# Later scatters, later low parts and shorter scaling turns in a chain of Fourier transform and two expert networks

## The chip, the cores and the metric

One core of a Trainium2 chip runs the whole program. The metric is the device time of one execution in microseconds. The kernel before took 698.27 us (median of three runs, 695.5 to 699.56).

## What is computed

```python
X = np.fft.fft(np.fft.fft(x, axis=1), axis=2).real          # x: (8, 3072, 256)
x = X.reshape(24576, 256)
# first network: 8 experts, weights w1 (8,256,1024), w2 (8,1024,256)
logits = x @ w_gate; P = np.exp(logits - logits.max())
for _ in range(8):
    P /= P.sum(1, keepdims=True) + 1e-09
    P /= P.sum(0, keepdims=True) + 1e-09
    P *= N / E
out = sum(P[:, e:e+1] * (np.maximum(x @ w1[e], 0.0) @ w2[e]) for e in range(8))
# second network, on out: each row goes to the expert of its largest logit
probs = softmax(out @ w_gate2); e = argmax
y[row] = probs[row, e] * (np.maximum(out[row] @ u1[e], 0) @ u2[e])
```

All is float32.

## The kernel before

The transform comes first (`fft_phase`) and leaves its rows in DRAM (`H`). Few rows have a P that is not zero in float32: `route1` finds them, and they are sorted into 30 tiles of 128 rows, three for each of the 8 experts (`CAP = 3`, tiles 0 to 23) and six spare tiles (`NFLAT = 6`, flat tiles 0 to 5) for what does not fit in three. A row that several experts want has copies; the flag `R["prim"]` marks the copy that counts in a column sum, `R["valid"]` the slots that hold a row.

The first network (`moe1`) goes through the experts e = 0 to 7. For each, `Moe.first` (matmuls on L890) makes the hidden layer of 384 rows in 8 groups m, each group in one of four PSUM buffers `ph`; `Moe.relu` takes it out with one ACT instruction (`hh`, L876) and one DVE instruction (`hl`, L427). `Moe.steps` (L923) is the second matrix, one tile t at a time. Every float32 matrix is split in a high part (ACT, L820) and a low part, the rest (`low`, DVE, L826), by `Moe.part`. The three-fold products of the high and low parts give the float32 result. `Moe.turn` transposes the rows of an expert (L843) and splits them as well (`xh` on ACT, `xl` on DVE, L418).

From e = 2 (`F0`) on each expert's stage also takes in one flat tile f = e - 2. Which expert a flat tile belongs to is known on the chip only, so `Free.weights` gathers its weights by index (L792): `fw` (1 MB, first matrix), `rawc` (1 MB, second matrix) and `gd`, three indirect DMAs issued by POOL. Each of the three has one buffer. `Moe.free_first` (L936, 32 matmuls) then reads `fw` at the start of stage e. In the order of POOL's queue the gathers for flat tile f stand at step 5 of stage f + 1.

The results of the first network are summed in DRAM (`acc`). `keep` copies a tile from PSUM into a buffer `y` (L1620), `add` writes it to its own rows by a plain DMA on SP's queue (L1631), and for the first tile of each expert after the first and for every flat tile puts a scatter in a list; `send` takes one entry of this list and issues an indirect DMA with addition on POOL's queue (L797, `acc<-y,Rapos` for a first tile, `acc<-y,Roidx` for a flat one). There are 13 of them. Each waits until the one in front of it has landed, as they touch the same rows. `ADDS` and `SENDS` say at which steps of a stage this happens. Steps are the slots of `Slots`: 0 to 7 behind the groups m of `first`, 8 to 10 in the flat tile's second matrix, 12 on in the three tiles. At (7, 6) and (7, 8) `most` sends what is left.

The scaling of P (`sinkhorn`) runs on DVE on one tile [128, 30, 8] beside stages 2 and 3, in steps that `STEPS` places in the slots: `start`, then eight turns (`cols`, `rows`) each followed by `sums` (L987), a matmul with a matrix of ones that adds the column sums `cs` over the partitions, and `end`, from which the weights `R["wt"]` come.

Behind stage 7 the logits of the sum are read back (`lg<-acc`, L1356), `route2` sorts the rows by expert for the second network, and the rows are gathered from `acc` (`grab2`, six gathers first, three per tile group). `warm` gives PE matmuls on zeros (L1263), so many as its argument says; `W3` are those within `route2` ahead of the matmuls on L550 that make the new row lists `R["gidx"]`. Then come the parts u, 0, 2 and u, 0, 3 of the second network's first expert, the first `turn` of it and `later`, nine small DVE instructions that end in the indices `R["frow"]` of the flat tiles. In `part` a list as last argument keeps the DVE low part, and for odd parts the next fetch of weights into the raw buffers, for later. The second network (`moe2`) has the same stages and writes its rows by indirect DMAs.

Of the kernel before, what the change touches and what calls it, by code (L numbers as in the profile page):

```python
# [12 lines left out]
ALU = mybir.AluOpType  # L13
# [4 lines left out]
NB, S, D, E, FF = 8, 3072, 256, 8, 1024  # L18
# [268 lines left out]
def _consts():  # L287
# [148 lines left out]
class Route:  # L436
# [364 lines left out]
class Moe:  # L801
# [7 lines left out]
    def part(self, r, i, eng, g=None, later=None):  # L809

        nc = self.nc
        if i < 2:
            h = self.w1.tile([128, FF], F32R, name="w1h")
            l = self.w1.tile([128, FF], F32R, name="w1l")
            hv, lv, rv = h, l, r
        else:
            h = self.w2.tile([128, 4, DG], F32R, name="w2h")
            l = self.w2.tile([128, 4, DG], F32R, name="w2l")
            hv, lv, rv = h[:, :, :D], l[:, :, :D], r.rearrange("p (m d) -> p m d", m=4)
        nc.scalar.activation(out=hv, in_=rv, func=AF.Copy)  # L820
        more = i >= 2 and g is not None
        if more:
            nc.scalar.activation(out=h[:, :, D:], in_=g, func=AF.Copy)

        def low():
            eng.tensor_tensor(out=lv, in0=rv, in1=hv.bitcast(F32), op=ALU.subtract)  # L826
            if more:
                eng.tensor_tensor(out=l[:, :, D:], in0=g, in1=h[:, :, D:].bitcast(F32), op=ALU.subtract)  # L828

        if later is None:  # L830
            low()
        else:
            later.append(low)
        return h, l
# [118 lines left out]
def sinkhorn(nc, K, R, pt, pool):  # L953

    o = Ops(nc)
    V = nc.vector
    T = lambda sh, dt=F32, name=None: pool.tile([128] + list(sh), dt, name=name)
    N8 = [128, NTL, 8]
    P, g, pr = T([NTL, 8], name="P"), T([NTL, 8], name="sg_"), T([NTL, 8], name="pr")
    rs, ri, rp, cs, bias = T([NTL], name="rs"), T([NTL], name="ri"), T([NTL], name="rp"), T([8], name="cs"), T([1], name="bias")  # L960
    bc = lambda a: a[:, :, None].to_broadcast(N8)

    def logits(j, X):
        s = slice(CAP * j, CAP * j + CAP)
        o.tt(g[:, s], X[:, :, 129:137], X[:, :, 273:281], ALU.add)
        o.tt(P[:, s], X[:, :, 265:273], R["sg"][:, s, None].to_broadcast([128, CAP, 8]), ALU.mult)
        o.tt(P[:, s], P[:, s], g[:, s], ALU.add)

    def start():
        o.ts(P, P, R["gm"], ALU.subtract)  # L970
        boltz(nc, o, P, g, bias)
        o.tt(P, P, bc(R["valid"]), ALU.mult)

    st = {}

    def rows(it):
        o.red(rs, P, ALU.add)
        o.stt(rs, rs, 1e-9 * (2.0 ** 64 if it == 0 else 1.0), rs, ALU.add, ALU.bypass)
        V.reciprocal(ri, rs)
        o.tt(rp, ri, R["prim"], ALU.mult)  # L980
        o.tt(pr, P, bc(rp), ALU.mult)
        o.red(cs, pr.rearrange("p t e -> p e t"), ALU.add)
        o.tt(P, P, bc(ri), ALU.mult)

    def sums():
        st["pm"] = pt.tile([128, 512], F32, name="pt")
        nc.tensor.matmul(st["pm"][:, 0:8], K["tri"][:, 128:256], cs, start=True, stop=True)  # L987

    def cols():
        o.ts(cs, st["pm"][:, 0:8], 1e-9, ALU.add, 1.0 / (NB * S // E), ALU.mult)  # L990
        V.reciprocal(cs, cs)
        o.tt(P, P, cs[:, None, :].to_broadcast(N8), ALU.mult)

    def end():
        cols()
        o.tt(pr[:, E * CAP:], P[:, E * CAP:], R["sel"], ALU.mult)
        o.red(R["wt"][:, E * CAP:], pr[:, E * CAP:], ALU.add)

        own = P.rearrange("p t e -> p (t e)")[:, :E * (8 * CAP + 1)].rearrange("p (e x) -> p e x", e=E)[:, :, 0:8 * CAP:8]
        o.stt(R["wt"][:, :E * CAP].rearrange("p (e c) -> p e c", e=E), own, 1.0, own, ALU.mult, ALU.bypass)  # L1000
# [12 lines left out]


# [120 lines left out]
F0 = 2  # L1135


def run(tc, ctx, A, out, H, acc, Ld, Pd, Gd, Zd):
    nc = tc.nc
    o = Ops(nc)  # L1140
    P = lambda st, n, b, **k: st.enter_context(tc.tile_pool(name=n, bufs=b, reuse_waits="tile", **k))
# [15 lines left out]
    R = {}  # L1157
# [43 lines left out]
    with tc.manual_schedule():  # L1201
# [27 lines left out]
        with ExitStack() as st:  # L1229
# [38 lines left out]
            def part(s, e, i, eng, later=None):  # L1268
                g = g2[:, e, 4 * (i - 2):4 * (i - 1)] if i > 1 and s == "w" else None
                k = s + "1122"[i], e  # L1270
                W.setdefault((s, e), {})[i] = moe.part(raw[k][:, i % 2], i, eng, g, later)

                def after():
                    raw.pop(k)
                    if (s, e, i) not in HOLD:
                        fetch()
                    if (s, e, i) == ("u", 0, 3):
                        fetch()

                if i % 2:  # L1280
                    after() if later is None else later.append(after)

            with ExitStack() as s1:
# [35 lines left out]
                X = {}  # L1319
# [41 lines left out]
            with ExitStack() as s1:  # L1361
                moe.xp = P(st, "xp2", 2, side="right")
                r2 = P(s1, "r2", 1)
                ring = P(s1, "r2a", 2)
                K["itx"] = r2.tile([128, NTL, NTL], BF16, name="itx2")
                K["irx"] = r2.tile([128, 128, max(CH2)], BF16, name="irx2")
                nc.scalar.activation(out=K["itx"], in_=rt.C("it")[:, :, None].to_broadcast([128, NTL, NTL]), func=AF.Copy)
                nc.scalar.activation(out=K["irx"], in_=rt.C("i128")[:, :, None].to_broadcast([128, 128, max(CH2)]), func=AF.Copy)

                def arrive(choose):  # L1370
                    pg = turned()
                    a, b = E * CAP - CAP + 1, E * CAP
                    o.tt(lg[:, a:b], pg[:, :8 * (b - a)].rearrange("p (t e) -> p t e", e=8),
                         R["wt"][:, a:b, None].to_broadcast([128, b - a, 8]), ALU.mult)
                    o.tt(lg[:, NTL - 1], lg[:, NTL - 1], last[:, D:DG], ALU.add)
                    choose(0, NTL)

                for _ in range(3):
                    zeros(2)
                later = route2(nc, rt, lg, K, R, r2, ring, arrive, more, Y2, lambda: warm(W3))  # L1380

                def grab2(j):
                    X[j] = xg.tile([128, CAP, HW], F32, name="Xg")
                    for i in range(CAP):
                        t = CAP * j + i
                        if j > 1:
                            for _ in range(2):
                                nc.gpsimd.memset(grow, 0.0)
                        gather(nc, X[j][:, i, :DW], acc, R["gidx"][:, t:t + 1])

                warm(W4)
                for j in (0, 1):
                    grab2(j)
                assert zat[0] == 97
                for i in (2, 3):
                    part("u", 0, i, nc.vector)
                xt = moe.turn(lambda i: X[0][:, i], lambda i: warm(3))
                later()
            fm, fi = kp.tile([128, 1], F32, name="fm"), kp.tile([128, 1], I32, name="fi")

# [34 lines left out]
SINK = (2, 4)  # L1435
STEPS = [0, 0, 4, 4, 8, 8, 12, 12, 16, 16, 20, 20, 24, 24, 28, 28, 32, 33]
FIRST = 7
ADDS, SENDS = (1, 3, 5, 7, 9, 13, 14, 15, 17, 19), (7, 13, 16, 19)

GRAB = ((0, 17, 4), (1, 4, 5), (2, 4, 9), (2, 14, 6), (3, 13, 7))  # L1440
PROB = ((0, 4, 0), (0, 1, 1), (1, 11, 8), (2, 6, 2), (3, 4, 3), (4, 4, 4), (4, 11, 9), (5, 4, 5), (6, 4, 6), (7, 5, 7))
BACK, BF, BL = [(8,), (8,), (8,), (8,), (4, 8), (2, 4, 6, 8)], ((2, 9), (4, 9), (6, 9)), 10
G2 = ("gg", "", "gggggg", "0l12g3gg", "ggww", "ggg")
Y2 = (8, 9)
W2, W3, W4 = 0, 16, 11


class Slots:
# [114 lines left out]
def moe1(nc, K, R, acc, moe, W, part, X, xg, Gd, w1f, w2f, xb, pt, zeros, zt, rest, ask, trash, warm, grow):  # L1563
    o = Ops(nc)
    V, G = nc.vector, nc.gpsimd
    sl = Slots()
    x = {}
# [101 lines left out]
    for j in range(10):  # L1669
        e, s = LOGIT[j]  # L1670
# [8 lines left out]
        if s in ADDS and (e, s) < (E - 1, 6):  # L1679
            sl.at(e, s, add)  # L1680

    for e in range(F0 + 1, E):
        for s in SENDS:
            if (e, s) < (E - 1, 6):
                sl.at(e, s, send)

    def most():
        while ys:
# [12 lines left out]
    f = ys[-1]  # L1701
# [103 lines left out]
```

## Time and profile before

| What | |
|---|---|
| Median of three runs | 698.27 us (695.5 to 699.56) |
| Profiled execution, its own time | 696.15 us |
| Its span in the trace | 694.2 us |
| PE (matmul) busy | 638.5 us, 92% |
| PE weight loads busy | 614.6 us, 89% |
| DVE busy | 440.1 us, 63% |
| ACT busy | 345.7 us, 50% |
| POOL busy | 221.5 us, 32% |
| DMA | 155.43 MB, mean 224 GB/s |

The rows further down come from this one profiled execution; its time is 1.95 us above its span and 2.12 us below the median. Busy shares are means over stages with different limits, so the places where PE stands idle say more than the shares.

### The profile page before, as it was taken

What the parts mean: (1) busy time and instruction counts of PE and PEld (TensorE: products, weight loads), DVE (VectorE), ACT (ScalarE), POOL (GpSimd) and SP (SyncE); (2) the same over time, 40 slices, a digit from 0 to 9 for tenths busy, and PEclk for the clock granted to TensorE, in tenths of its full rate; (3) what the DMA queues carried; (4) which work ended last, traced back from release to release, by engine and by line L of the source; (5) the groups of instructions that cost most, each with busy time, mean ns of one, the idle gap of its engine ahead of it and who ended that gap; (6) DMA issues with size and microseconds to landing.
All of it is one profiled execution on the core that took longest, in us unless ns stands there. A gap on an engine that the chain in (4) does not pass through costs nothing. (4 is left out here: it accounts for less than half of the span.)

```text
span 694.2 us, 12596 instructions
## 1 busy us (share of the span) xinstructions
PE 638.5 (92%) x4749; PEld 614.6 (89%) x4749; DVE 440.1 (63%) x985; ACT 345.7 (50%) x687; POOL 221.5 (32%) x343
## 2 busy tenths in 40 slices
PE   7999999999998997994969987998799999999996
PEld 4989999999988987994969987998499999999996
DVE  4397777777238947849996753856466546645750
ACT  1365667666655114544433652753145545654651
POOL 0002221122110088821010533412357575332332
PEclk8599999999999779997979999999889999999999
DMA  8989999996889148897546769776655385557500
GB/s 215 266 222 287 305 289 273 298 290 231 304 290 382 64 113 271 295 213 302 182 155 162 219 233 315 232 260 189 206 171 189 114 311 205 184 197 258 194 36 34
DMA packets 67039, 155.43 MB, mean 224 GB/s; under 512 B 17891, under 2 KB 35787, under 8 KB 59164
## 3 DMA queue, kind: packets, MB, share of 16 engines
q1 hardware_dynamic: 56812, 114.73, 52.9%
q0 software_dynamic: 9840, 39.45, 17.9%
q8 instruction: 39, 0.64, 0.4%
q10 hardware_dynamic: 320, 0.37, 0.2%
q14 instruction: 28, 0.23, 0.1%
HBM read 104.00 MB, written 50.44 MB: 222 GB/s over the span
## 5 line engine op out<-in xcount | busy, mean ns | idle before, releaser
L427 DVE SCALAR_TENSOR_TENSOR hl<-ph,hh 128x384 fp32r<-128x384 f32 (+1 forms) x164 | 85.8, 542 | 104.5 <-ACT hh L876 101.7
L923 PE MATMUL py<-w2h,hh 128*128 128x264 f32 (+1 forms) x480 | 141.0, 294 | 0.0
L923 PE MATMUL py<-w2l,hh 128*128 128x264 f32 (+1 forms) x480 | 138.6, 289 | 1.5 <-DVE w2l L826 0.8
L923 PE MATMUL py<-w2h,hl 128*128 128x264 f32 (+1 forms) x480 | 138.2, 288 | 0.0
L876 ACT ACTIVATE hh<-ph 128x384 fp32r<-128x384 f32 (+1 forms) x164 | 76.6, 481 | 62.3 <-PE ph L936 31.9
L923 PEld LDWEIGHTS py<-w2l,hh 128*128 128x128 f32 x480 | 93.6, 195 | 2.2 <-DVE w2l L828 1.2
L923 PEld LDWEIGHTS py<-w2h,hh 128*128 128x128 f32 x480 | 93.5, 195 | 0.0
L923 PEld LDWEIGHTS py<-w2h,hl 128*128 128x128 f32 x480 | 93.4, 195 | 0.0
L73 PEld LDWEIGHTS pp<-ca,w 96*128 96x128 f32 x512 | 64.7, 208 | 4.4 <-DVE w L159 3.5
L890 PE MATMUL ph<-xh,w1h 128*128 128x384 f32 x256 | 67.4, 344 | 1.1 <-DVE nf L422 0.9
L73 PE MATMUL pp<-ca,w 96*128 96x96 f32 x512 | 65.6, 291 | 3.0 <-DVE w L159 3.0
L890 PE MATMUL ph<-xl,w1h 128*128 128x384 f32 x256 | 65.2, 335 | 0.0
L75 ACT ACTIVATE at<-pp 128x384 f32<-128x384 f32 x64 | 52.3, 858 | 25.8 <-PE pp L73 24.9
L890 PE MATMUL ph<-xh,w1l 128*128 128x384 f32 x256 | 65.1, 335 | 0.0
L125 POOL TENSOR_TENSOR lc<-hd 128x32 f32<-128x32 f32 (+1 forms) x25 | 9.8, 393 | 168.7 <-ACT hd L121 150.9
L797 POOL DMA_INDIRECT out_dram<-y,Rorow x30 | 33.7, 1123 | 84.4 <-ACT hh L876 29.7
L936 PE MATMUL ph<-Xg,fw 128*128 128x128 f32 x384 | 48.4, 287 | 6.6 <-DMA fw<-in_w_dram,Rfrow 6.6
L936 PEld LDWEIGHTS ph<-Xg,fw 128*128 128x128 f32 x384 | 47.2, 203 | 7.0 <-DMA fw<-in_w_dram,Rfrow 4.2
L90 PE MATMUL pp<-cb,t 128*128 128x128 f32 x368 | 48.2, 278 | 0.6 <-DVE t L83 0.6
L890 PEld LDWEIGHTS ph<-xh,w1h 128*128 128x128 f32 x256 | 45.4, 189 | 3.4 <-DVE nf L422 1.2
L83 DVE COPY t<-pp 128x512 f32<-128x512 f32 (+2 forms) x56 | 33.0, 609 | 23.7 <-PE pp L81 23.7
L890 PEld LDWEIGHTS ph<-xl,w1h 128*128 128x128 f32 x256 | 46.2, 188 | 0.1
(328 smaller groups left out, 1283.5 us busy)
## 6 DMA issues: line engine op xcount, KB each, us to landing
out_dram<-zt SPq DMA_DIRECT2D x48, 512.0 KB
H<-hd SPq DMA_DIRECT2D x24, 562.0 KB
xa<-in_xa_dram SPq DMA_DIRECT2D x32, 384.0 KB
xm<-in_xm_dram SPq DMA_DIRECT2D x32, 384.0 KB
rawa<-in_w_dram SPq DMA_DIRECT2D x8, 1024.0 KB
rawb<-in_w_dram SPq DMA_DIRECT2D x8, 1024.0 KB
rawa<-in_u_dram SPq DMA_DIRECT2D x8, 1024.0 KB
rawb<-in_u_dram SPq DMA_DIRECT2D x8, 1024.0 KB
```

The source lines that it names most:

```text
L73: nc.tensor.matmul(p[:M, i], lhs(4 * h + i), ca, start=True, stop=True)
L75: nc.scalar.activation(out=at[:M, :, :, s0:s0 + 4].rearrange("m g j s -> m s g j"), in_=p[:M], func=AF.Copy)
L83: nc.vector.tensor_copy(out=t[:, :n, :M], in_=p[:, :n, :M])
L90: nc.tensor.matmul(p[:M, i * 128:(i + 1) * 128], t[:, i, :M], cb[:, (g0 + i) * 128:(g0 + i + 1) * 128], start=True, stop=True)
L125: nc.gpsimd.tensor_tensor(out=lc[:np_, :n], in0=hd[:np_, :, 129:137], in1=hd[:np_, :, 273:281], op=ALU.add)
L427: self.nc.vector.scalar_tensor_tensor(out, a, s, b, op0, op1)
L797: nc.gpsimd.indirect_dma_start(out=dst, out_offset=bass.IndirectOffsetOnAxis(ap=idx, axis=0), in_=src, in_offset=None, **kw)
L876: self.nc.scalar.activation(out=a[:, :n], in_=p[:, :n], func=AF.Relu)
L890: self.nc.tensor.matmul(p[:, :N], w, xx, start=(i == 0), stop=(i == 5))
L923: self.nc.tensor.matmul(p[:, :nd], c, W[2 + m // 4][w][:, m % 4, :nd], start=(m == 0 and i == 0), stop=(m == 7 and i == 2))
L936: self.nc.tensor.matmul(p[:, m * 128:(m + 1) * 128], w[:, k, (m0 + m) * 128:(m0 + m + 1) * 128], x[:, k, i * 128:(i + 1) * 128], start=(k ...
```

## The change

Three things change. In `sinkhorn` the tile gets a ninth column, which holds the small constant that was added by an instruction of its own, and eight more rows `Q`. The expert tiles are stored in the order (tile in expert, expert), so that the first tiles of all experts are rows 0 to 7; only these are multiplied by `prim` into `Q`, and the column sums go over rows 8 to 37. `start` copies `valid` into the new order. In the second network's beginning the low parts of u, 0, 2 and u, 0, 3 are kept back until behind the first `turn`, and `W3` goes from 16 to 13. `SENDS` becomes a table by stage.

```diff
+    PE_ = T([NTL + E, 9], name="P")
+    P, Q = PE_[:, :NTL, :8], PE_[:, NTL:, :8]
+    g, pr, vp = T([NTL, 8], name="sg_"), T([NFLAT, 8], name="pr"), T([NTL], name="vp")
...
     def logits(j, X):
         s = slice(CAP * j, CAP * j + CAP)
-        o.tt(g[:, s], X[:, :, 129:137], X[:, :, 273:281], ALU.add)
...
+        d = slice(j, E * CAP, E) if j < E else s
+        o.tt(g[:, d], X[:, :, 129:137], X[:, :, 273:281], ALU.add)
...
     def start():
+        o.cp(vp[:, :E * CAP].rearrange("p (c e) -> p e c", c=CAP), R["valid"][:, :E * CAP].rearrange("p (e c) -> p e c", c=CAP))
+        o.cp(vp[:, E * CAP:], R["valid"][:, E * CAP:])
+        V.memset(PE_[:, :, 8:], 1e-9 * 2.0 ** 64)
         o.ts(P, P, R["gm"], ALU.subtract)
         boltz(nc, o, P, g, bias)
-        o.tt(P, P, bc(R["valid"]), ALU.mult)
+        o.tt(P, P, bc(vp), ALU.mult)
...
     def rows(it):
-        o.red(rs, P, ALU.add)
-        o.stt(rs, rs, 1e-9 * (2.0 ** 64 if it == 0 else 1.0), rs, ALU.add, ALU.bypass)
+        o.red(rs, PE_[:, :NTL], ALU.add)
+        if it == 0:
+            V.memset(PE_[:, :, 8:], 1e-9)
         V.reciprocal(ri, rs)
-        o.tt(rp, ri, R["prim"], ALU.mult)
-        o.tt(pr, P, bc(rp), ALU.mult)
-        o.red(cs, pr.rearrange("p t e -> p e t"), ALU.add)
         o.tt(P, P, bc(ri), ALU.mult)
+        o.tt(Q, P[:, :E], R["prim"][:, 0:E * CAP:CAP, None].to_broadcast([128, E, 8]), ALU.mult)
+        o.red(cs, PE_[:, E:, :8].rearrange("p t e -> p e t"), ALU.add)
...
+                held = []
                 for i in (2, 3):
-                    part("u", 0, i, nc.vector)
+                    part("u", 0, i, nc.vector, held)
                 xt = moe.turn(lambda i: X[0][:, i], lambda i: warm(3))
+
+                for f in held:
+                    f()
                 later()
...
-ADDS, SENDS = (1, 3, 5, 7, 9, 13, 14, 15, 17, 19), (7, 13, 16, 19)
+ADDS = 1, 3, 5, 7, 9, 13, 14, 15, 17, 19
+SENDS = {4: (7, 12), 5: (7, 11, 15), 6: (7, 11, 15, 19), 7: (1, 3)}
...
-W2, W3, W4 = 0, 16, 11
+W2, W3, W4 = 0, 13, 11
...
-    for e in range(F0 + 1, E):
-        for s in SENDS:
-            if (e, s) < (E - 1, 6):
-                sl.at(e, s, send)
+    for e in SENDS:
+        for s in SENDS[e]:
+            sl.at(e, s, send)
```

## Rows read from the trace of the kernel before

**Rows 1.** Waits of PE: line, releaser: us in total, times, longest us.

```profile
PE pt L987 <- DVE cs L433: 10.7, 2, 8.6
PE ph L936 <- DMA fw<-in_w_dram,Rfrow: 6.6, 2, 4.0
PE pt L987 <- DVE xl L418: 4.1, 2, 3.2
```

**Rows 2.** The chain that ended last: start us, length us, what.

```profile
390.29 10.73 DMA fw<-in_w_dram,Rfrow
...
401.15 5.36 PE ph L936 x32
...
431.06 5.47 PE ph L936 x32
...
471.10 4.52 DMA acc<-y,Rapos
...
497.42 5.53 DMA Xg<-acc,Rgidx
...
506.68 8.44 PE ph L890 x48
...
543.14 3.57 PE ph L936 x32
```

**Rows 3.** Timeline of POOL: start, us, line, op, tiles, count, idle time and releaser.

```profile
377.40 1.62 POOL L797 DMA_INDIRECT acc<-y,Rapos  x1 [27.14 <-DVE hl L427]
382.17 3.04 POOL L797 DMA_INDIRECT acc<-y,Roidx  x1 [3.14 <-DVE x L1591]
388.28 1.70 POOL L797 DMA_INDIRECT acc<-y,Rapos  x1 [3.08 <-DVE y L422]
...
398.69 1.61 POOL L797 DMA_INDIRECT acc<-y,Roidx  x1 [4.10 <-DMA acc<-y,Rapos]
...
444.01 1.44 POOL L792 DMA_INDIRECT gd<-Gd,Rfrow  x1 [0.30 <-issue]
```

**Rows 4.** DVE: groups of tiles P and pr (ns min/median/max), then a turn's timeline.

```profile
L433 DVE TENSOR_REDUCE rs<-P x8: 403/403/403, 319.5 to 362.8; 128x30 f32<-128x240 f32 x8
L418 DVE TENSOR_TENSOR pr<-P,rp x8: 407/408/409, 320.8 to 364.1; 128x240 f32<-128x240 f32 x8
L433 DVE TENSOR_REDUCE cs<-pr x8: 578/592/623, 321.2 to 364.5; 128x8 f32<-128x240 f32 x8
L418 DVE TENSOR_TENSOR pr<-P,Rsel x1: 209/209/209, 369.3 to 369.3; 128x48 f32<-128x48 f32 x1
...
357.32 0.15 DVE L424 TENSOR_SCALAR cs<-pt 128x8 f32<-128x8 f32 x1
...
358.62 0.19 DVE L427 SCALAR_TENSOR_TENSOR rs<-rs 128x30 f32<-128x30 f32 x1
...
360.70 1.01 DVE L418 TENSOR_TENSOR xl<-pt,xh 128x384 fp32r<-128x384 f32 x2
```

**Rows 5.** Second network's beginning: timelines of PE, DVE, POOL, SP; gathers as a group.

```profile
487.55 3.63 PE L1263 MATMUL py<-zb 128*128 128x512 bf16 x16
499.09 0.43 PE L843 MATMUL pt<-ident,Xg 128*128 128x128 f32 x2 [2.29 <-DMA Xg<-acc,Rgidx]
...
495.01 2.35 DVE L826 TENSOR_TENSOR w2l<-rawb,w2h 128x1024 fp32r<-128x1024 f32 x2
505.74 1.02 DVE L418 TENSOR_TENSOR xl<-pt,xh 128x384 fp32r<-128x384 f32 x2 [8.38 <-ACT xh L846]
508.40 0.56 DVE L427 SCALAR_TENSOR_TENSOR hl<-ph,hh 128x384 fp32r<-128x384 f32 x1
...
495.36 1.76 POOL L792 DMA_INDIRECT Xg<-acc,Rgidx  x1 [13.39 <-DVE Rgidx L418]
...
497.39 0.34 SPq L1198 DMA_DIRECT2D rawb<-in_u_dram  x1
...
L792 POOL DMA_INDIRECT Xg<-acc,Rgidx x30: 949/956/1756, 495.4 to 588.3; - x30
```

More of the change, by code (lines that the diff above doesn't have):

```diff
@@ L957, in sinkhorn @@
     T = lambda sh, dt=F32, name=None: pool.tile([128] + list(sh), dt, name=name)
+    PE_ = T([NTL + E, 9], name="P")
+    P, Q = PE_[:, :NTL, :8], PE_[:, NTL:, :8]
+    g, pr, vp = T([NTL, 8], name="sg_"), T([NFLAT, 8], name="pr"), T([NTL], name="vp")
+    rs, ri, cs, bias = T([NTL], name="rs"), T([NTL], name="ri"), T([8], name="cs"), T([1], name="bias")
     N8 = [128, NTL, 8]
-    P, g, pr = T([NTL, 8], name="P"), T([NTL, 8], name="sg_"), T([NTL, 8], name="pr")
-    rs, ri, rp, cs, bias = T([NTL], name="rs"), T([NTL], name="ri"), T([NTL], name="rp"), T([8], name="cs"), T([1], name="bias")
     bc = lambda a: a[:, :, None].to_broadcast(N8)
@@ L964, in logits @@
         s = slice(CAP * j, CAP * j + CAP)
-        o.tt(g[:, s], X[:, :, 129:137], X[:, :, 273:281], ALU.add)
-        o.tt(P[:, s], X[:, :, 265:273], R["sg"][:, s, None].to_broadcast([128, CAP, 8]), ALU.mult)
-        o.tt(P[:, s], P[:, s], g[:, s], ALU.add)
+        d = slice(j, E * CAP, E) if j < E else s
+        o.tt(g[:, d], X[:, :, 129:137], X[:, :, 273:281], ALU.add)
+        o.tt(P[:, d], X[:, :, 265:273], R["sg"][:, s, None].to_broadcast([128, CAP, 8]), ALU.mult)
+        o.tt(P[:, d], P[:, d], g[:, d], ALU.add)
     def start():
+        o.cp(vp[:, :E * CAP].rearrange("p (c e) -> p e c", c=CAP), R["valid"][:, :E * CAP].rearrange("p (e c) -> p e c", c=CAP))
+        o.cp(vp[:, E * CAP:], R["valid"][:, E * CAP:])
+        V.memset(PE_[:, :, 8:], 1e-9 * 2.0 ** 64)
         o.ts(P, P, R["gm"], ALU.subtract)
         boltz(nc, o, P, g, bias)
-        o.tt(P, P, bc(R["valid"]), ALU.mult)
+        o.tt(P, P, bc(vp), ALU.mult)
     st = {}
     def rows(it):
-        o.red(rs, P, ALU.add)
-        o.stt(rs, rs, 1e-9 * (2.0 ** 64 if it == 0 else 1.0), rs, ALU.add, ALU.bypass)
+        o.red(rs, PE_[:, :NTL], ALU.add)
+        if it == 0:
+            V.memset(PE_[:, :, 8:], 1e-9)
         V.reciprocal(ri, rs)
-        o.tt(rp, ri, R["prim"], ALU.mult)
-        o.tt(pr, P, bc(rp), ALU.mult)
-        o.red(cs, pr.rearrange("p t e -> p e t"), ALU.add)
         o.tt(P, P, bc(ri), ALU.mult)
+        o.tt(Q, P[:, :E], R["prim"][:, 0:E * CAP:CAP, None].to_broadcast([128, E, 8]), ALU.mult)
+        o.red(cs, PE_[:, E:, :8].rearrange("p t e -> p e t"), ALU.add)
     def sums():
@@ L995, in end @@
         cols()
-        o.tt(pr[:, E * CAP:], P[:, E * CAP:], R["sel"], ALU.mult)
-        o.red(R["wt"][:, E * CAP:], pr[:, E * CAP:], ALU.add)
-        own = P.rearrange("p t e -> p (t e)")[:, :E * (8 * CAP + 1)].rearrange("p (e x) -> p e x", e=E)[:, :, 0:8 * CAP:8]
+        o.tt(pr, P[:, E * CAP:], R["sel"], ALU.mult)
+        o.red(R["wt"][:, E * CAP:], pr, ALU.add)
+        own = PE_[:, :E * CAP].rearrange("p (c e) x -> p c (e x)", c=CAP)[:, :, 0:9 * E:10].rearrange("p c e -> p e c")
         o.stt(R["wt"][:, :E * CAP].rearrange("p (e c) -> p e c", e=E), own, 1.0, own, ALU.mult, ALU.bypass)
```

## The prediction, made before the changed kernel was built

> **What bounds the kernel now.** PE is busy nearly all the time, so the time is PE's work plus PE's idle gaps; the question for each edit is which gap it closes. I read the waits of PE first, to see who opens the gaps [rows 1], then the chain that ended last, to see which of them the end hangs on and how fast PE runs behind them [rows 2], then the timelines of the engines that open them. Three places touch the change. In stages 2 and 3 the column sums wait for DVE, 10.7 us in two waits for `cs` and 4.1 us in two for the pt buffer that `xl` frees [rows 1]. At the start of stages 5 and 6 L936 waits 2.6 and 4.0 us for the gathered `fw` [rows 1], and its 32 matmuls then take 5.36 and 5.47 us where stages without a wait need 3.57 [rows 2]. At the start of the second network the transposes wait for the gathers from `acc` [rows 2, 5].
>
> **Scatters behind the gathers.** POOL works in order. Before, three scatters stand in front of the `fw` gather of stage 5; they are issued at 377.40, 382.17 and 388.28 [rows 3], each behind the landing of the one in front, and the gather follows only at 390.29 and lands 10.7 us later [rows 2]. In front of stage 6's gather stand four more. With the new table one scatter stands in front of the first gather, two in front of the second. So the first can go at 377.40 + 1.62 + 0.3, about 379.3, 11 us earlier, and needs 2.6; its buffer is read for the last time one stage (some 24 us) before the wait at 398.5, plus 3.6, so near 378. The second waits for its buffer only, that is for L936 of stage 5; some 24 us then lie ahead of its use, against a transfer of 10.7. Both waits go: 2.6 + 4.0 = 6.6. The 32 matmuls go back to 3.57: 1.8 + 1.9 = 3.7. Together 10.3 us.
>
> What is late next: the number of scatters is the same, 13, so they move back. Between the last gather's `gd` (444.01 [rows 3]) and the scatter of stage 7's first tile (471.10 [rows 2]), which the read of the logits waits for, stand two scatters before and five after. Both ends of this stretch of 27.1 us hang on PE's stages and move with it. It holds 1.44 + 0.3 + 5 s, where s is the distance of two scatters: up to 5.1 us it costs nothing. The rows show 4.8 (377.40 to 382.17), 6.1 (382.17 to 388.28) and 10.4 (388.28 to 398.69, with two gathers of 1 MB behind it on the same queue) [rows 3]. DVE and the queue are quieter late in stage 6, so I take 4.8 for four and 7.3 for the first, which shares the queue with the gathers: 28.2, a loss of 1.1 us (0 to 5). Nothing else reads `acc` in between, and 15 `y` buffers cover the scatters that wait longer. Sum: -9.2 (-10.3 to -5).
>
> **Shorter turns.** A turn takes DVE 3.38 us (357.32 to 360.70 [rows 4]). It loses two instructions of the 0.19 us kind (one is shown), and the 240-wide product of 0.41 becomes one of 64, for which the row of 48 (0.21) is nearest: I take 0.23. The row sum reads 270 instead of 240 elements, 0.40 becomes 0.45. The sum over the tiles still reads 240 elements (rows 8 to 37), so its 0.59 stays. So DVE is free 0.5 us earlier per turn. But P times `ri`, which stood behind `cs`, now stands ahead of it, so `cs` itself comes only 0.1 us earlier. `start` gains two copies and a memset, and the first turn a memset: by the 0.19 rows some 0.5 us (0.2 to 0.6), on the path, since the first wait, 8.6 us, is DVE's. So: +0.4 at the first wait; the second turn gives 0.5 to `xl` and 0.7 of its wait goes; in stage 3, where DVE works without a pause, two turns lie ahead of the `xl` at 360.70, 2 x 0.5. Sum: 0.4 - 0.7 - 1.0 = -1.3 (+0.4, only the added instructions, to -2). The other turns lie beside PE's work and give nothing. The nine-wide rows could slow the instructions a little; the bound of +0.4 takes that in.
>
> **Low parts behind the transposes.** `W3` takes three of 16 warm matmuls away, 3.63 x 3/16 = 0.7 us, from in front of the matmuls that make the row lists, which sit on the chain. The two low parts run on DVE from 495.01, just when POOL issues the first gather; this one takes 1.76 us, the longest of thirty with a median of 0.96 [rows 5]. When they end, `rawb` is free and SP starts 1 MB into it at 497.39 [rows 5]; the second gather, issued at 497.42, needs 5.53 us [rows 2], while the first landed 1.97 us behind the end of its issue (497.12 to 499.09 [rows 5]). Behind the change DVE and SP are silent here: 494.7 + 0.96 + 1.97 = 497.6 for the first gather, the next two 1.26 apart, the third at 500.1. Before, 3.72 us lay between the second landing and L890 at 506.68 [rows 2], for two tiles; one tile's half behind the third landing gives 502.0 for L890, 4.7 us earlier. If the gathers take longer (the far end is 5.53 each again) only the 0.7 stays. The price: DVE has been idle for 8.38 us when `xl` comes [rows 5], and now 2.35 us of low parts stand between `xl` and the first `hl`, which came 1.72 us behind L890's start. So it ends 1.72 + 2.35 + 0.56 = 4.6 us behind it; with four ph buffers the fifth group wants to start after 4 x 1.05 = 4.2, a wait of 0.4 (up to 1.3 if L890 starts sooner). Then DVE catches up, 0.56 against 1.05 per group. The fetch into `rawb` starts some 7 us later; it is used in the next stage, 20 us on. Sum: -4.3 (-4.5 to +0.5).
>
> The rows show that a low part of two SBUF operands lengthens an issue on POOL from 0.96 to 1.76 us [rows 5]. The Trainium skill, page "SBUF — State Buffer", section "Who interferes with whom", says otherwise: a `tensor_tensor` with both inputs in SBUF gets in the way of GpSimd's reads only, and descriptor writing should not notice it. By that rule the 0.8 us of the first issue would have another cause and stay. I go by the row; the rule is a rival below.
>
> **The sum.** -9.2 - 1.3 - 4.3 = -14.8. Profiled: 696.15 - 14.8 = 681.4. That execution is 2.1 us below the median of the runs, so the median after is 698.27 - 14.8 = 683.5.
>
> **Rivals.** (a) The scatters pile up: with 6.1 us each the last one comes 5.1 late, 4.0 more than in the sum, 687.5. For it speaks that two of the three distances are above 5.1; against it that the longest has two gathers behind it. (b) The other side, the same list at its worst: from 8.3 us a scatter on, the stretch is 15.9 too long and takes back all gains; with 10.4 each it is 26.6 too long, 709. It decides at the read of the logits. Against it: 10.4 was seen once, between gathers, and at most one of the five stands so. (c) The change doesn't do what it says for the second gather: the scatter at (4, 12) waits for writes that SP issues late, holds POOL, and stage 6 waits as before, 5.9 us: 689.4. Some 20 us of room speak against it. (d) The low parts backfire: the gathers stay at 5.5 us for another cause, and the first `hl` is late: 0.7 won, 1.2 lost, 688.3. The `rawb` transfer, which starts in the very moment, speaks against it. (e) Gathers are issued no faster without the low parts: 0.8 of the sum is lost, 684.3. By the Trainium skill's port rule this one would hold.
>
> **How the numbers follow.** Forecast 0.53 (679 to 686); a 0.20; b 0.05; c 0.08; d 0.07; e 0.07. The range takes in a, c, d, e and the lower ends of the terms (-10.3, -2 and -4.5 give 681.5, less the scatter of the medians, 3 to 4 us): 677.5 to 692. About 0.5%, 3.5 us, is what a measurement of this kernel can tell from no change. All but b end faster; a and d together, with s near 7, can meet within that bound. Faster 0.88, same 0.06, slower 0.06.
>
> **What would show it.** Right: the `fw` gather of stage 5 issued near 378 and no wait on L936, its 32 matmuls at 3.6 us; five scatters between the last `gd` and the scatter of stage 7's first tile, the last of them landing just ahead of it; first gather from `acc` issued in under 1 us, the second landing about 3 us behind its issue, L890 a small wait at its fifth group; DVE's turn 2.9 us. Wrong: the scatter of stage 7's first tile issued several us behind its `y`; a wait on L936 in stage 6; the wait for the first column sums longer than 9.2 us; a transpose still waiting 2.8 us for the second gather.

## The result: 0.8% slower where 2% faster was forecast

The changed kernel takes 701.76 us (median of 20 runs, 697.8 to 707.94), the kernel before 696.63 (20 runs beside them). The ratio is 1.0079, with a 95% interval of 1.0055 to 1.0104. The profiled execution of the changed kernel took 702.99 us, its span is 700.8 (before 694.2).

The waits of PE in the changed kernel (line, releaser: us in total, times, longest):

```profile
PE pt L459 <- DVE cd L433: 14.5, 2, 12.7
PE pt L995 <- DVE cs L433: 11.6, 2, 9.6
PE ph L936 <- DMA fw<-in_u_dram,Rfrow: 5.2, 1, 5.2
...
PE pt L995 <- DVE xl L418: 2.8, 1, 2.8
...
PE ph L890 <- DVE hl L427: 1.1, 2, 0.8
...
PE pt L843 <- DMA Xg<-acc,Rgidx: 0.2, 1, 0.2
```

In the kernel before, L459 waited so:

```profile
PE pt L459 <- DVE cd L433: 4.0, 2, 2.2
```

Against [rows 1] the two waits for the first network's `fw` (6.6 us) are gone, as the change wants. Two others have come: 12.7 us at L459 (2.2 before), the count in front of the second network, which needs the logits read back from `acc`; and 5.2 us for the second network's own `fw`, where before there was none.

To see where the time went I cut the run at instructions that both kernels have and took the distances between their starts on PE's timeline. All stretches but the first begin where the one before ends:

| Stretch, us | before | after | difference |
|---|---|---|---|
| start to L936 of stage 2 | 300.2 | 303.1 | +2.9 |
| to L936 of stage 4 (turns) | 72.9 | 70.9 | -2.0 |
| to L890 of stage 6 (both `fw` waits) | 63.2 | 52.9 | -10.3 |
| to the count on `cd`, L459 | 46.8 | 57.3 | +10.5 |
| to L890 of the second network (low parts) | 23.1 | 19.0 | -4.1 |
| to L936 of its flat tile 0 | 36.9 | 37.8 | +0.9 |
| to L936 of its flat tile 2 | 47.8 | 55.5 | +7.7 |
| to the end | 103.5 | 104.3 | +0.8 |

The first row holds of all edits only the logits' new places in `sinkhorn`'s tile. Over the eleven kernels profiled here it went from 299.7 to 303.1 us with the new turns and from 300.2 to 305.1 without, so it says nothing of the change. The three places that were edited gained about what was forecast. Two places behind them gave it back.

**The first loss** is on POOL. Its timeline in the changed kernel (start, us, line, op, tiles, count, idle time before it and releaser):

```profile
380.29 1.62 POOL L797 DMA_INDIRECT acc<-y,Rapos  x1 [25.63 <-DVE Xg L1585]
382.21 1.12 POOL L792 DMA_INDIRECT fw<-in_w_dram,Rfrow  x1 [0.30 <-PE ph L890]
...
397.92 1.58 POOL L797 DMA_INDIRECT acc<-y,Rapos  x1 [7.96 <-issue]
403.35 1.01 POOL L792 DMA_INDIRECT fw<-in_w_dram,Rfrow  x1 [3.73 <-PE ph L936]
411.87 0.97 POOL L792 DMA_INDIRECT rawc<-in_w_dram,Rfrow  x1 [7.52 <-DVE w2l L828]
...
432.41 2.22 POOL L797 DMA_INDIRECT acc<-y,Roidx  x1 [4.46 <-DMA acc<-y,Rapos]
434.93 1.18 POOL L792 DMA_INDIRECT fw<-in_w_dram,Rfrow  x1 [0.30 <-issue]
...
437.69 1.64 POOL L792 DMA_INDIRECT gd<-Gd,Rfrow  x1 [0.30 <-issue]
439.63 2.42 POOL L797 DMA_INDIRECT acc<-y,Rapos  x1 [0.31 <-issue]
450.84 1.59 POOL L797 DMA_INDIRECT acc<-y,Roidx  x1 [8.67 <-DMA acc<-y,Rapos]
458.33 2.19 POOL L797 DMA_INDIRECT acc<-y,Rapos  x1 [5.79 <-issue]
463.76 1.55 POOL L797 DMA_INDIRECT acc<-y,Roidx  x1 [3.24 <-ACT hh L876]
468.29 1.55 POOL L797 DMA_INDIRECT acc<-y,Rapos  x1 [2.98 <-issue]
472.97 1.56 POOL L797 DMA_INDIRECT acc<-y,Rapos  x1 [3.02 <-ACT y L1633]
```

The gathers for stages 5 and 6 now go early, at 382.21 and 403.35 ([rows 2]: 390.29 for the first before), and L936 of these stages, at 399.33 and 423.50, no longer waits. But behind the last gather trio (`fw`, `rawc` and `gd`, the last at 437.69) stand five scatters, and the one of stage 7's first tile goes out at 472.97. SP had issued the plain write of the same tile long before:

```profile
461.11 0.32 SPq L1644 DMA_DIRECT2D acc<-y  x1
```

So the scatter was held for nearly 12 us. The distances of the five, 439.63 to 472.97, are 11.2, 7.5, 5.4, 4.5 and 4.7. On DVE, the instruction that adds the logits of these rows shows what it costs (the changed kernel, then the kernel before):

```profile
480.97 0.17 DVE L418 TENSOR_TENSOR lg<-lg,y 128x8 f32<-128x8 f32 x1 [12.19 <-DMA lg<-acc]
```

```profile
479.73 0.17 DVE L418 TENSOR_TENSOR lg<-lg,y 128x8 f32<-128x8 f32 x1 [1.66 <-DMA lg<-acc]
```

It waits 12.19 us for the read of `acc`, where it waited 1.66 us before; all of the route behind it, and PE's wait at L459, hang on it.

**The second loss** is in the second network. The chain that ended last, in the changed kernel (start, us, what):

```profile
555.82 6.67 DMA out_dram<-y,Rorow
...
562.59 0.48 ACT y L1750
...
563.24 0.96 POOL out_dram L797
...
564.51 5.77 DMA fw<-in_u_dram,Rfrow
...
570.32 6.07 PE ph L936 x32
```

The gather of flat tile 1's `fw` stands on POOL behind six output scatters, which go out one by one, each behind the landing of the one ahead. It goes at 564.51. The same queue in the kernel before (POOL's timeline again; L936 of flat tile 1 came at 566.86 and did not wait):

```profile
509.20 0.94 POOL L792 DMA_INDIRECT fw<-in_u_dram,Rfrow  x1 [5.77 <-DVE hl L427]
...
527.84 0.99 POOL L797 DMA_INDIRECT out_dram<-y,Rorow  x1 [0.30 <-issue]
...
555.37 0.98 POOL L792 DMA_INDIRECT fw<-in_u_dram,Rfrow  x1 [0.30 <-PE ph L890]
```

In the changed kernel PE waits 5.2 us, and the 32 matmuls behind the wait take 6.07 us in place of 3.57 [rows 2]. The granted clock tells why: it was 0.61 on the mean while they ran, so that part of them ran at the lower of the two levels (1.2 GHz), and 1.00, the upper level (2.4 GHz), in the 32 matmuls of flat tile 0, ahead of which PE had not waited. The rows where this begins, POOL first and then DVE, in the changed kernel:

```profile
496.96 1.02 POOL L792 DMA_INDIRECT Xg<-acc,Rgidx  x1 [13.75 <-DVE Rgidx L418]
498.28 0.98 POOL L792 DMA_INDIRECT Xg<-acc,Rgidx  x1 [0.30 <-issue]
...
509.01 0.94 POOL L792 DMA_INDIRECT fw<-in_u_dram,Rfrow  x1 [4.74 <-DVE hl L427]
...
528.25 1.98 POOL L797 DMA_INDIRECT out_dram<-y,Rorow  x1 [0.30 <-ACT w2h L820]
```

```profile
504.22 2.35 DVE L826 TENSOR_TENSOR w2l<-rawb,w2h 128x1024 fp32r<-128x1024 f32 x2
...
508.03 0.17 DVE L430 CAST Rfrow<-wr 128x6 int32<-128x6 f32 x1
...
528.15 1.23 DVE L826 TENSOR_TENSOR w2l<-rawb,w2h 128x1024 fp32r<-128x1024 f32 x1
```

The gathers from `acc` are quick now (1.02 and 0.98 us, 1.76 for the first in [rows 5]). But `later`, which makes `Rfrow`, is written behind the two held low parts: `Rfrow` is ready at 508.2, 4.9 us behind L890 (503.31), and POOL's first `fw` gather of this network starts 5.7 us behind L890, where it was 3.1 us before. In all eleven kernels this gather starts 0.8 us behind `Rfrow`. So what follows in POOL's queue is some 2.6 us later against PE, and the first output scatter meets a low part of DVE (528.15) and takes 1.98 us to issue instead of 0.99.

### The profile page after: what moved, and what is told of

Same layout as the page of the kernel before. It is cut to its first block, busy times and chain, and to the rows that moved or that the text cites. A ratio compares the mean times of both kernels' runs of the same rounds, so it can differ in the third digit from the quotient of the medians.

```text
span 700.8 us, 12568 instructions
## 1 busy us (share of the span) xinstructions
PE 634.2 (90%) x4742; PEld 610.2 (87%) x4746; DVE 436.4 (62%) x973; ACT 345.9 (49%) x687; POOL 220.0 (31%) x343
## 3 DMA queue, kind: packets, MB, share of 16 engines
q1 hardware_dynamic: 56812, 114.73, 52.5%
q0 software_dynamic: 9840, 39.45, 18.1%
## 5 line engine op out<-in xcount | busy, mean ns | idle before, releaser
L890 PE MATMUL ph<-xh,w1h 128*128 128x384 f32 x256 | 67.5, 344 | 2.2 <-DVE hl L427 1.1
L73 PEld LDWEIGHTS pp<-ca,w 96*128 96x128 f32 x512 | 61.5, 199 | 4.9 <-DVE w L159 4.2
L73 PE MATMUL pp<-ca,w 96*128 96x96 f32 x512 | 62.2, 281 | 3.7 <-DVE w L159 3.7
L890 PE MATMUL ph<-xl,w1h 128*128 128x384 f32 x256 | 65.2, 336 | 0.0
L890 PE MATMUL ph<-xh,w1l 128*128 128x384 f32 x256 | 65.1, 335 | 0.0
L936 PE MATMUL ph<-Xg,fw 128*128 128x128 f32 x384 | 47.4, 284 | 5.2 <-DMA fw<-in_u_dram,Rfrow 5.2
L936 PEld LDWEIGHTS ph<-Xg,fw 128*128 128x128 f32 x384 | 46.3, 200 | 5.4 <-DMA fw<-in_u_dram,Rfrow 5.4
L890 PEld LDWEIGHTS ph<-xh,w1h 128*128 128x128 f32 x256 | 44.9, 188 | 5.4 <-DVE hl L427 2.7
L890 PEld LDWEIGHTS ph<-xl,w1h 128*128 128x128 f32 x256 | 46.3, 188 | 0.1
L890 PEld LDWEIGHTS ph<-xh,w1l 128*128 128x128 f32 x256 | 46.3, 188 | 0.0
## 6 DMA issues: line engine op xcount, KB each, us to landing
rawa<-in_u_dram SPq DMA_DIRECT2D x8, 1024.0 KB, 10.5
```

The lines of the kernel that those rows point to most:

```text
L73: nc.tensor.matmul(p[:M, i], lhs(4 * h + i), ca, start=True, stop=True)
L890: self.nc.tensor.matmul(p[:, :N], w, xx, start=(i == 0), stop=(i == 5))
L936: self.nc.tensor.matmul(p[:, m * 128:(m + 1) * 128], w[:, k, (m0 + m) * 128:(m0 + m + 1) * 128], x[:, k, i * 128:(i + 1) * 128], start=(k ...
```

## Experiments

Two theories had to be tested: that the pile-up of scatters brings the wait for the logits, and that the late `Rfrow` brings the late `fw` in the second network. The rival in both: that the change as a whole shifts the stages and the losses belong to no single part. The first four kernels take the parts apart.

**The turns alone.** `sinkhorn` as in the change, the rest as before:

```diff
...
-        o.tt(rp, ri, R["prim"], ALU.mult)
-        o.tt(pr, P, bc(rp), ALU.mult)
-        o.red(cs, pr.rearrange("p t e -> p e t"), ALU.add)
         o.tt(P, P, bc(ri), ALU.mult)
+        o.tt(Q, P[:, :E], R["prim"][:, 0:E * CAP:CAP, None].to_broadcast([128, E, 8]), ALU.mult)
+        o.red(cs, PE_[:, E:, :8].rearrange("p t e -> p e t"), ALU.add)
...
```

> The shorter scaling turns alone; scatters, low parts and W3 as before. Theory: the turns are not to blame. By the traces of before and after, stages 2 and 3 together (first L936 of stage 2 to first L936 of stage 4) shrink from 72.9 to 70.9 us, so 2 us are won; the 3 us by which the changed kernel reached stage 2 late are noise of the transform. Expected 2 us less than before. Rival: the nine-wide rows and the new order slow DVE from the first logits on, stage 2 is reached 3 us later again, and the kernel is 1 to 3 us slower than before.

Ratio 0.9957 (0.993 to 0.9984), 3.0 us faster. The stretch from L936 of stage 2 to that of stage 4 takes 67.9 us, and stage 2 is reached at 299.9, not late: the rival fails.

**The low parts alone**, held, with `W3 = 13`:

```diff
+                held = []
                 for i in (2, 3):
-                    part("u", 0, i, nc.vector)
+                    part("u", 0, i, nc.vector, held)
                 xt = moe.turn(lambda i: X[0][:, i], lambda i: warm(3))
+
+                for f in held:
+                    f()
                 later()
...
-W2, W3, W4 = 0, 16, 11
+W2, W3, W4 = 0, 13, 11
```

> The low parts behind the first transposes and W3 = 13 alone; turns and scatters as before. Theory: the start of the second network gets 3.2 us shorter (first matmul of the row lists' counts to the second turn of the second network), as between the traces of before and after, and nothing else moves, so 3 us less than before. Rival: the fetch into rawb that comes later, or what it pushes, makes the gather of fw in stage 3 of the second network late (wait of 5 us on L936 there, matmuls behind it 2.5 us slower): then 4 us more than before.

Ratio 1.0065 (1.0033 to 1.0098). The beginning of the second network is 4.4 us shorter (18.7 us from L459 to L890), and the new wait is there by itself:

```profile
PE ph L936 <- DMA fw<-in_u_dram,Rfrow: 5.1, 1, 5.1
```

So the second loss belongs to this part. The time is that of the rival; whether the cause is the late fetch into `rawb`, which the rival names, or `later`, this run can't tell.

**The scatters alone:**

```diff
-ADDS, SENDS = (1, 3, 5, 7, 9, 13, 14, 15, 17, 19), (7, 13, 16, 19)
+ADDS = 1, 3, 5, 7, 9, 13, 14, 15, 17, 19
+SENDS = {4: (7, 12), 5: (7, 11, 15), 6: (7, 11, 15, 19), 7: (1, 3)}
...
-    for e in range(F0 + 1, E):
-        for s in SENDS:
-            if (e, s) < (E - 1, 6):
-                sl.at(e, s, send)
+    for e in SENDS:
+        for s in SENDS[e]:
+            sl.at(e, s, send)
```

> The new table of scatters alone; turns, low parts and W3 as before. Theory: no wait on L936 in stages 5 and 6 (10.3 us won), but the scatter of stage 7's first tile is issued 10 to 12 us behind its y, as two scatters stand behind 2 MB of gathers and take 11 us each instead of 5; PE waits 12 us for the counts of the row lists instead of 2. Expected 0 to 1 us more than before. Rival: the scatters in the changed kernel were late by chance, distances of 5 us are the rule, and this is 8 to 10 us less than before.

Ratio 1.0023 (0.9989 to 1.0058). No wait for `fw`, 53.1 us from L936 of stage 4 to L890 of stage 6 (63.2 before), and then 57.6 us to L459 (46.8 before):

```profile
PE pt L459 <- DVE cd L433: 14.8, 2, 12.9
```

The first loss belongs to this part, and it eats the whole gain.

**Turns and low parts, the scatters as before.** Both edits above in one kernel, the first places kept:

```diff
-ADDS = 1, 3, 5, 7, 9, 13, 14, 15, 17, 19
-SENDS = {4: (7, 12), 5: (7, 11, 15), 6: (7, 11, 15, 19), 7: (1, 3)}
+ADDS, SENDS = (1, 3, 5, 7, 9, 13, 14, 15, 17, 19), (7, 13, 16, 19)
...
```

> The changed kernel with the old table of scatters. Theory: the late scatters cost what the waits on fw gave, so without them 2 + 3.2 = 5 us less than before, and the waits on L936 in stages 5 and 6 are back (2.6 and 4.0 us). Rival: the turns or the low parts bring the wait of 5 us for fw into stage 3 of the second network; then it is 2 to 3 us more than before.

Ratio 1.0012 (0.9986 to 1.0039): neither the 5 us less of the theory nor, clear of noise, the 2 to 3 us more of the rival. The wait for the second network's `fw` is there again, 3.2 us. It stood in all three kernels with the low parts behind the transposes and ahead of `later`, and in none of the three without (before and the two single parts).

Now each cause was taken away by itself. **The low parts behind `later`:** as the second kernel, but the row lists first.

```diff
+                later()
                 for f in held:
                     f()
-                later()
```

> The low parts behind the transposes again, alone and with 13 warm matmuls, but the row lists that `later` makes (with `frow`, on which the gather of the second network's first fw waits) stand ahead of the two held low parts instead of behind them. Theory: in the change the two low parts put `frow` 2.6 us further behind the first L890 (5.7 us in place of 3.1), the nine reads from acc and the serial chain of output scatters behind it shift by the same, meet other work, and the gather for flat tile 1 comes late. With the order turned, the fw gather is issued 3.1 us behind L890, the first output scatter 22 us behind it (25 with the low parts alone), flat tile 1's matmuls don't wait (L936 of flat tile 0 to that of flat tile 1 in 23.9 us, not 29), and what the low parts gained at the beginning is kept: ratio 0.994 to 0.998. Rival 1: the late gather comes from the 1 MB into rawb, which starts some 7 us later than before and still does: the wait of 5 us stays, ratio 1.004 to 1.008. Rival 2: the three warm matmuls fewer are at fault: likewise 1.004 to 1.008.

Ratio 0.9953 (0.992 to 0.9987). POOL's timeline in this kernel, where L890 starts at 499.6:

```profile
503.03 1.13 POOL L792 DMA_INDIRECT fw<-in_u_dram,Rfrow  x1 [2.45 <-ACT hh L876]
...
522.23 0.99 POOL L797 DMA_INDIRECT out_dram<-y,Rorow  x1 [0.30 <-issue]
...
549.73 0.98 POOL L792 DMA_INDIRECT fw<-in_u_dram,Rfrow  x1 [0.30 <-PE ph L890]
```

`Rfrow` is ready 2.6 us behind L890 (4.9 in the changed kernel), the first gather follows L890 in 3.4 us, the first output scatter takes 0.99 us and goes 22.6 us behind L890, the gather for flat tile 1 goes at 549.73, 11.5 us ahead of its L936 at 561.2: from flat tile 0 to flat tile 2 PE needs 47.8 us, as before. The transfer into `rawb` still starts late here (at 504.56, 5.0 us behind L890) and three warm matmuls are still missing, so neither rival holds. This part is now worth 3.3 us.

**Three scatters fewer:** the scatters' new places alone, without the adding scatters of tiles 9, 12 and 15.

```diff
-                if not alone(t):
+                if not alone(t) and t not in (9, 12, 15):
                     sq.append((acc[:r], R["apos"][:, t // CAP:t // CAP + 1], y))
```

> The scatters' new places alone, and the adding scatters of tiles 9, 12 and 15 left out (so those rows of acc lack their second expert's part; the row lists of the second network then differ in content, not in shape). Theory: the new wait of 12.7 us for the logits' read in front of the second network is the pile-up of the scatters, each of which waits for the landing of the one ahead; with three fewer the scatter of stage 7's first tile goes as soon as its tile is written, the wait falls to about 2 us, and the 10 us saved at stages 5 and 6 come through: ratio 0.985 to 0.990 (0.998 to 1.006 with all scatters). Rival: the logits' read is late for another cause (DVE's own work, the slower kernel of stage 7 having less time in front of it): the wait stays at 10 us or more and the ratio near 1.002.

Ratio 0.9877 (0.9827 to 0.9927). PE's waits for `cd`, and then DVE's addition of the logits:

```profile
PE pt L459 <- DVE cd L433: 3.8, 2, 2.0
```

```profile
472.28 0.17 DVE L418 TENSOR_TENSOR lg<-lg,y 128x8 f32<-128x8 f32 x1 [1.48 <-DMA lg<-acc]
```

With three scatters less in the queue the wait is back at 2.0 us, and the gain at stages 5 and 6 comes through. The pile-up is the cause. This run takes bytes away as well as links of the chain, so the next one leaves the bytes as they are.

**One scatter into the gap.** In the changed kernel POOL stands still from 404.4 to 411.87, since the buffer `rawc` is still read by DVE. The list is kept whole, the turns and the low parts are as before, and one scatter is put there:

```diff
-SENDS = {4: (7, 12), 5: (7, 11, 15), 6: (7, 11, 15, 19), 7: (1, 3)}
+SENDS = {4: (7, 12, 16), 5: (7, 11, 15), 6: (7, 11, 15, 19), 7: (1,)}
```

> The scatters' new places alone, with one more place behind (4, 12) and one fewer in stage 7: {4: (7, 12, 16), 5: (7, 11, 15), 6: (7, 11, 15, 19), 7: (1,)}. In the change POOL stands still for 8 us in front of stage 6's rawc gather, since its buffer is still being read; one scatter fits into that gap. Theory (the chain of scatters is what sets the logits' read): the one scatter less between stage 7's gathers and the scatter of its first tile brings that scatter forward by one distance, 4.7 us; the wait in front of the second network falls from 12.9 to about 8, ratio 0.994 to 0.998. Rival: the queue is bound by its total bytes and not by the chain, so the scatter in the gap only slows the gathers beside it: the wait at L936 in stage 6 comes back or the wait for the logits stays at 12 us or more, ratio 1.000 to 1.006.

Ratio 0.996 (0.9926 to 0.9993). POOL's timeline, and the wait:

```profile
407.61 2.05 POOL L797 DMA_INDIRECT acc<-y,Roidx  x1 [6.19 <-DMA acc<-y,Rapos]
409.96 1.01 POOL L792 DMA_INDIRECT fw<-in_w_dram,Rfrow  x1 [0.30 <-PE ph L890]
...
469.64 1.56 POOL L797 DMA_INDIRECT acc<-y,Rapos  x1 [2.98 <-issue]
```

```profile
PE pt L459 <- DVE cd L433: 9.8, 2, 8.0
```

One scatter goes in the gap at 407.61, the gather behind it still is not late, and the wait falls from 12.9 to 8.0, by one distance.

**All three parts, mended.** The changed kernel with the last order of `later` and the last table.

```diff
+                later()
                 for f in held:
                     f()
-                later()
...
-SENDS = {4: (7, 12), 5: (7, 11, 15), 6: (7, 11, 15, 19), 7: (1, 3)}
+SENDS = {4: (7, 12, 16), 5: (7, 11, 15), 6: (7, 11, 15, 19), 7: (1,)}
```

> The whole change with its two faults mended: the row lists of `later` ahead of the two held low parts, and the scatter table {4: (7, 12, 16), 5: (7, 11, 15), 6: (7, 11, 15, 19), 7: (1,)}. Theory: the three parts add up, since each acts in another stretch: shorter turns 3.0 us (0.9957 alone), low parts in the new order 3.3 us (0.9953), scatters with one in the gap 2.8 us (0.996); together 9 us, ratio 0.983 to 0.991, no wait for fw in either network, a wait of about 8 us for the logits. Rival: the parts feed each other (an earlier stage 7 waits longer for the same scatters, which hang on the chain of landings and not on PE), so that what the turns give is lost in front of the logits' read: ratio 0.990 to 0.996 and a wait of 10 us or more there.

686.48 us (six runs), ratio 0.9864 (0.9817 to 0.991), so the three parts add up. There is no wait for `fw` in either network, and at L459 remains:

```profile
PE pt L459 <- DVE cd L433: 9.7, 2, 7.9
```

**The same without the scatters' new places:**

```diff
-ADDS = 1, 3, 5, 7, 9, 13, 14, 15, 17, 19
-SENDS = {4: (7, 12, 16), 5: (7, 11, 15), 6: (7, 11, 15, 19), 7: (1,)}
+ADDS, SENDS = (1, 3, 5, 7, 9, 13, 14, 15, 17, 19), (7, 13, 16, 19)
...
```

> The shorter turns and the low parts in the new order, the scatters where they stood before. Theory: 3.0 + 3.3 = 6.3 us, ratio 0.988 to 0.994, with the two waits for fw at stages 5 and 6 as before and a wait of about 2 us for the logits. This tells what the scatters' new places are worth beside the other two: if the mended whole is faster than this by 2 us or more they bring something, if it is within 1 us they only move the wait from stages 5 and 6 to the logits' read.

689.09 us, ratio 0.9918 (0.9886 to 0.9951), with

```profile
PE pt L459 <- DVE cd L433: 4.5, 2, 2.6
PE ph L936 <- DMA fw<-in_w_dram,Rfrow: 4.3, 1, 4.3
```

Both beat the kernel before. Between the two the medians differ by 2.6 us, above the 2 us named ahead; drawing again from the six and the twelve times puts the difference between 0.3 and 6.5 us. So the times point to a gain by the table, but its size is open: the spans of the profiled executions are 683.0 and 683.7 us. Of the two `fw` waits one is gone here even with the old places (also in the earlier kernel with turns and low parts), so there is less left for the scatters to win. What takes it away is not shown: the turns alone and the low parts alone each kept both waits.

The stretches in which the kernels differ, in us, from PE's timeline (columns as in the table above):

| Kernel | stage 2 to 4 | both `fw` waits | to L459 | to L890, second network | flat tile 0 to 2 |
|---|---|---|---|---|---|
| before | 72.9 | 63.2 | 46.8 | 23.1 | 47.8 |
| after | 70.9 | 52.9 | 57.3 | 19.0 | 55.5 |
| turns alone | 67.9 | 62.5 | 46.9 | 23.2 | 47.8 |
| low parts alone | 70.5 | 63.3 | 46.7 | 18.7 | 56.0 |
| scatters alone | 70.5 | 53.1 | 57.6 | 24.4 | 47.8 |
| turns and low parts | 70.0 | 59.9 | 47.0 | 18.2 | 51.2 |
| low parts behind `later` | 70.3 | 62.7 | 46.9 | 18.7 | 47.8 |
| three scatters fewer | 70.9 | 52.9 | 46.6 | 21.7 | 47.8 |
| one scatter into the gap | 71.8 | 53.1 | 52.6 | 23.1 | 47.8 |
| all three, mended | 69.9 | 53.0 | 52.5 | 18.8 | 47.8 |
| mended, old scatters | 68.1 | 59.2 | 47.3 | 18.1 | 47.8 |

Read down the columns: both large losses, and the gains at the `fw` waits and in front of L890, each go with one edit. Two cells do not fit, 59.9 and 59.2, where turns and low parts together take one `fw` wait away. In the first column the kernels with the new turns (67.9 to 70.9) and without (70.3 to 72.9) overlap.

## Why the prediction was wrong

**The gain of the scatters' new places was right:** 10.3 us were forecast for the two waits and the slow matmuls, and the stretch lost 10.3 us. The 32 matmuls of stages 5 and 6 take 3.73 us each on PE's timeline of the changed kernel, at a granted clock of 1.00; before, they took 5.36 and 5.47 [rows 2] at a mean of 0.69. The 3.57 of the forecast is the chain's reading; on the timeline of the kernel before, such a group without a wait takes 3.74.

**The step that failed first is the distance of two scatters,** in "what is late next". I saw the right place, five scatters between the last gathers and that of stage 7's first tile, but I took 7.3 us for the first and 4.8 for the others, 26.5 us from the first to the fifth behind it; it was 33.3. The first, behind the 2 MB of gathers, needs 11.2 (the 10.4 of [rows 3] was the nearest row, and I shared the difference instead of taking it), the second 7.5. That is 6.8 us. "DVE and the queue are quieter late in stage 6" rested on no row: beside the slow scatters, the second too, the trace shows plain transfers on the other queue (last section), and the sum had none of them. The rest came ahead of that stretch: I let its beginning move with PE's stages, but the third scatter of stage 5, at 432.41, held the last trio until 434.93, while L936, whose end frees `fw`, had started at 423.50. The `gd` at 437.69 is 6.3 us earlier than in [rows 3], PE's stage 6 is 9.3 us earlier; 3.0 us are lost there. With the 1.1 us of the forecast that makes 6.8 + 3.0 + 1.1 = 10.9, against 10.5 measured; behind the scatter of stage 7's first tile some 0.6 us less are needed than before. So "both ends of this stretch hang on PE's stages and move with it" is wrong: the beginning hangs on POOL's own chain of landings. Apart from the gap in front of `rawc` and a shorter one for the `fw` buffer at 403.35, the chain runs without a break from 380.29 to 472.97, with 11 distances and three trios between, and PE's gain of 10 us could not shorten it. From `gd` to the scatter of stage 7's first tile it took 35.3 us, 8.2 more than the 27.1 of the prediction. Rival (a) had this at 5.1 us, rival (b) at 15.9 or more; with the 3.0 lost ahead of it, the loss takes the whole gain back.

**The low parts did at the beginning what was forecast:** first issue 1.02 us, a wait of 0.2 us for the second landing, 4.1 us gained to L890 (4.7 forecast), and 0.77 us lost at the fifth group (0.4 forecast, 1.3 the bound). The 0.4 came from a reading: 506.68 is where the chain's piece begins, while PE's timeline has the first L890 at 506.11, so the first `hl` came 2.3 us behind it and not 1.72, and the same sum gives about 1.0. **The second step that failed is a term that was missing:** I priced what the two low parts put in front of the first `hl`, but not what they put in front of `later`, which stands behind them, and so in front of POOL's queue. Its price is the 7.7 us of the stretch from flat tile 0 to flat tile 2, 5.2 in the wait and 2.5 in the matmuls behind it. In the kernel before, the gather went at 555.37 and PE came at 566.86; with a transfer of 5.77 (the chain above) 5.7 us of room were left. But 2.6 us of shift grew on the way: from L936 of flat tile 0 to the gather it took 12.4 us before (543.0 to 555.37) and 23.4 after (541.1 to 564.51), 11 us more, since the scatters were slower one by one: three of their issues took 1.98, 1.81 and 1.96 us (before, the longest was 1.80 and the next 1.47), and two of the last distances were 6.1 and 7.4 us, where before they were 3.3 and 3.6. The slow issues fall on low parts of DVE. The 7.4 has a cause in the trace: SP issues a fetch of 1 MB into `rawb` at 556.95, just as POOL is issuing the scatter of 555.82, and the scatter's first packet comes 3.25 us behind the end of its issue; in the kernel before, all six scatters were through by 556.2, ahead of that fetch (558.88), and the last three began 0.6 us behind their issues. ACT's `y` (562.59, the chain above) and so the last scatter waited for that landing. How much of the 11 us each of these brought was not tested by a run of its own. My rival (d) looked for the backfire in the first `hl`, and so missed it.

**The turns went as forecast,** if anything better. The changed kernel's DVE timeline of one turn:

```profile
361.25 0.16 DVE L424 TENSOR_SCALAR cs<-pt 128x8 f32<-128x8 f32 x1
...
362.13 0.43 DVE L433 TENSOR_REDUCE rs<-P 128x30 f32<-128x270 f32 x1
...
363.42 0.23 DVE L418 TENSOR_TENSOR P<-P,Rprim 128x64 f32<-128x64 f32 x1
363.68 0.57 DVE L433 TENSOR_REDUCE cs<-P 128x8 f32<-128x240 f32 x1
364.18 1.01 DVE L418 TENSOR_TENSOR xl<-pt,xh 128x384 fp32r<-128x384 f32 x2
```

361.25 to 364.18 are 2.93 us (3.38 in [rows 4], 2.9 forecast); the 64-wide product takes the 0.23, the row sum over 270 elements 0.43 (0.45). Stages 2 to 4 take 69.4 us on the mean of the five kernels with the new turns and 71.2 on the mean of the six without: 1.8 us, against 1.3 forecast. That the first wait for `cs` gets 0.4 us longer can't be told: it went from 6.4 to 9.6 us in kernels with the new turns and from 6.8 to 8.6 in those without.

**The range** ended at 692. Two terms that fail at once stood in the prediction only as (a) with (d), which was put at no change. The chance of 0.06 for slower rested on 8.3 us a scatter being needed from all five; the mean of the five was 6.7, and the other loss did the rest.

By rival (e) the first issue would have stayed at 1.8 us. It is 1.02 in all six kernels in which the two low parts were moved away; with them in place it is 1.75 or 1.76 in four kernels and 1.10 in the turns alone. Over all eleven traces, output scatters and gathers from `acc` took above 1.3 us to issue in 87 of the 219 cases that fell together with a low part of L826, and in none of 441 others. These rows go against the sentence of the Trainium skill, page "SBUF — State Buffer", section "Who interferes with whom", which infers that a `tensor_tensor` with both inputs in SBUF leaves descriptor writing alone. Whether it is the writing that is held up, or POOL's reading of the row indices, no run separates.

## What to carry to other kernels

A chain of transfers that wait for each other's landing is a resource with a time of its own: add up its distances over all of its length, those beside large transfers, on whatever queue, at their full length, before an edit takes away a wait that gave it time. When work is moved behind something on one engine, list what stands behind the new place in program order, down to the last queue that reads its result: here nine tiny instructions were carried along, and 2.6 us on DVE became 7.7 on PE. Filling a gap that the queue has anyway (one scatter while POOL waits for a buffer) was worth a whole distance (12.9 to 8.0 us at L459); the later places without it brought nothing that can be told from noise (1.0023).

## What the runs showed of the hardware

In the changed kernel a scatter of 128 rows to `acc` needs 4.5 to 5.4 us to the next where the DMA queues are quiet or nearly so, and 9.7 to 11.2 us right behind the two gathers of 1 MB. The packets in its trace show where the time goes. The scatter issued at 439.63 was done with its issue at 442.05, but its 1060-byte packets run only from 446.0 to 449.6. The gathers' packets of 8192 bytes on the same queue run from 436.8 to 447.5, and plain transfers moved 249 GB/s on the other queue between the issue's end and the last packet.

The gathers ahead are not needed for such a wait. The scatter of 397.92 has no packet of a gather beside it, and its first one comes 2.9 us behind the end of its issue, with plain transfers at 325 GB/s; that of 450.84 waits 2.1 us so, at 228 GB/s. The three of 463.76 to 472.97, beside which no plain transfer runs, wait 0.57 us each. Over the eleven traces, 56 scatters to `acc` had no gather and under 30 GB/s of plain transfers beside them, and all wait 0.57 or 0.58 us. The 48 with plain transfers of 100 GB/s or more and no gather wait 0.57 to 3.9 us, 2.1 in the median; the 31 with packets of gathers as well 0.9 to 4.8, 3.6 in the median. So an indirect DMA of 132 KB can wait 4 us and more for its first packet beside large transfers of either queue; here these were in part weights that nobody needed yet (L936 reads the gathered `fw` of 434.93 only at 458.90). How the wait of the scatter of 439.63 divides between the two queues was not separated.
